# A fused attention and spatial-gating kernel: a new cost table and rank table for its list scheduler, some engines chosen by it, and weights converted in PSUM

## The chip, the cores and the metric

The kernel runs on one core of a Trainium2 chip. The core has TensorE (PE, matmuls into PSUM), VectorE (DVE), ScalarE (ACT), GpSimd (POOL) and SyncE (SP, which here issues every load and store). The metric is the time of one execution on the device in microseconds. Times before: 559.58 us as the median of three runs, from 556.43 to 561.42.

## The reference

Inputs are q, k and v of 4 batches x 8 heads x 768 tokens x 64, and the weights of an MLP with a spatial gate. Everything is float32 on the reference's side; some weights arrive as float64.

```python
def _attn_ref(q, k, v, n_global, n_local):          # 8 global keys, a window of 96
    scores = scale * np.matmul(q, k.transpose(0, 1, 3, 2))
    ...
    keep = is_global | is_local
    ...
    scores = np.where(keep, scores + bias, -1e9)     # bias = -slope[h] * distance
    a = np.exp(scores - np.max(scores, axis=-1, keepdims=True))
    return np.matmul(a / (np.sum(a, axis=-1, keepdims=True) + 1e-09), v)

def _moe_ref(x, w_in, w_spatial, b_spatial, w_out):  # x: 4 x 768 x 512
    h = np.maximum(x @ w_in, 0.0)                    # 512 -> 1024
    u, v = h[..., :512], h[..., 512:]
    v_n = (v - mu) / np.sqrt(var + 1e-06)            # over the last axis
    v_s = np.einsum('ts,bsd->btd', w_spatial, v_n) + b_spatial[None, :, None]
    return (u * v_s) @ w_out
```

## The kernel before

Work is cut into 24 blocks of 128 tokens, six to a batch. A block's attention (`scores` and `values`) needs only the block's own keys, those of the block before it, and up to 32 global keys which are copied over the first rows of a ring of keys (`kring`) and of values (`vring`). Per block and pair of heads: score matmuls into PSUM tile `s`; one DVE instruction adds the bias, evicts to `pr` and finds the extreme `mn`; ACT takes the exponential and its sum; DVE takes the reciprocal `rc`; POOL multiplies `pr` by it; PE transposes `pr` into `p`; ACT and DVE evict it as a high and a low part (`pth`); PE multiplies by the values into `ops`; ACT and DVE sum the parts into `c`, and ACT and POOL write the MLP's input as high part `xth` and low part `xtl`. Batch 0 does its attention matmuls in full float32 without such parts, each as two records in the profile.

The MLP works on chunks: `mlp_v` per 128 tokens (12 matmuls of 512 columns, ReLU, normalisation, parts `vnh` and `vnl`), `mlp_u` per 256 tokens (48 of 256 columns), `mlp_s` (72 of 256 columns, the spatial product; DVE adds `b_bc`, the gate product with `u` follows, then parts `gh` and `gl`) and `mlp_o` (24 of 512 columns, eviction, store). All its matmuls go to two PSUM banks, `m`. Each is a sum of three products of high and low parts.

The float64 weights are loaded raw and converted during batch 0 (`split_weights`, 12 tiles of 128x512): the bits of the upper word are rebuilt as a float by ACT and DVE, the lower word is added, ACT rounds the high part `hi`, and two more steps make `lo`. Before, this works in SBUF buffers (`raw`, `rawh`, `ev`) and the last two steps (`wsub`, `wadd`) run on POOL.

The program is not issued as it is written. A `Recorder` collects every call with its engine, what it reads and writes and a token (which step of which block or batch). `link` finds the dependences, `cost` gives each call a busy time and a time until its result counts, and `plan` is a list scheduler: at each step it takes the engine that is free first and gives it the ready call of the lowest rank. The rank is a due time from the token (`keys.get(token, default)`); before, `KEYS` is empty and the defaults hold. The engine of each kind of call stands in `CFG` ('a' ACT, 'v' DVE, 'p' POOL). The five queues that come out are then executed in order, each waiting for the others by semaphores. Every recorded call has line 35 in the profile (39 after the change), so one goes by tiles. Input loads and stores all pass through SP's one queue.

The program also holds a second, general path behind a branch that these inputs do not take.

Of the kernel before, what the change touches and what calls it, by code (L numbers as in the profile page):

```python
# [26 lines left out]
CFG = {'bias1': 'pppppppp', 'bias2': 'pppppppp', 'S': [['I01', 'A'], ['I00', 'T00', 'T01', 'A', 'V00', 'B00'], ['T02', 'T03', 'A', 'V01', 'U00'], ['T04', 'T05', 'A', 'V02'], ['Q00', 'Q01', 'A', 'V03', 'U01'], ['Q02', 'Q03', 'A', 'V04']], 'T': [['V15', 'U12', 'A'], ['G10', 'O10', 'A'], ['G11', 'O11', 'A'], ['G12', 'O12', 'V00', 'V01', 'U00', 'A'], ['V02', 'A'], ['V03', 'U01', 'A', 'V04']], 'END': ['V05', 'U02', 'G00', 'O00', 'G01', 'O01', 'G02', 'O02'], 'whi': 'a', 'wsub': 'p', 'wadd': 'p', 'wth': 'a', 'wtl': 'p', 'vhi': 'p', 'vlo': 'p', 'qhi': 'a', 'qlo': 'v', 'khi': 'a', 'klo': 'v', 'pth0': 'aaaa', 'x0h': 'aa', 'x0l': 'vv', 'pth': 'aaaa', 'xh': 'aa', 'c1': 'aa', 'xl': 'pppp', 'vnh': 'a', 'vnl': 'p', 'gm': 'pp', 'gh': 'aa', 'gl': 'pv', 'o': 'aa', 'norm0': 'pppppppp', 'norm': 'pppppppp', 'wp': 0, 'vrn': 'v', 'dup': 1, 'fold': '', 'xb': 1, 'div': 'a', 'rows': 'p', 'xf0h': 'a', 'xf0l': 'v', 'xdiv': 'v', 'xbh': 'a', 'xbl': 'p', 'b_rawqk': 1, 'b_ev': 3, 'b_raw': 1, 'b_pr': 10, 'b_pth': 2, 'b_c1': 3, 'b_ps_s': 2, 'b_ps_p': 2, 'b_ps_o': 2, 'b_ps_m': 2}  # L27
# [3 lines left out]
class Op:  # L31
    __slots__ = ("eng", "call", "args", "kw", "reads", "writes", "token", "num", "preds", "busy", "late", "port", "seq", "real")
# [21 lines left out]
class Recorder:  # L54
# [13 lines left out]

    def add(self, engine, call, args, kw):
        op = Op()  # L70
        op.eng, op.call, op.args, op.kw, op.token, op.real = engine.name, call, args, kw, self.now, engine.real
# [37 lines left out]
SIZE = {BF16: 1}  # L109
seen = {}  # L110
# [3 lines left out]
def extent(ap):  # L114

    t = ap.tensor
    key = t.name, ap.offset, tuple(tuple(x) for x in ap.ap), str(ap.dtype)
    if key not in seen:
        u = SIZE.get(ap.dtype, 2)
        row = 1  # L120
        for x in t.shape[1:]:
            row *= x
        row = row * SIZE.get(t.dtype, 2) // u
        p0, f0 = divmod(ap.offset, row)
        bits = 1
# [25 lines left out]

def cost(op):

    n = elements(op.writes[0])
    src = op.reads[0] if op.reads else op.writes[0]
    psum = any(in_psum(x) for x in op.reads + op.writes[:1])
    if op.eng == "tensor":
        if op.call == "transpose":
            return 109, 260, False
        n = elements(op.kw["rhs"])  # L160
        if op.kw["rhs"].dtype == F32:
            return 4 * max(n, 128) * .422, 4 * n * .422 + 170, False
        return {128: 111, 256: 120, 512: 228}[n], n * .417 + 175, False
    if op.eng == "sync":
        size = n * 4 * list(op.writes[0].ap)[0][1]
        return 560, 2200 + size * .0035, False
    if op.eng == "scalar":
        t = 60 + .82 * n if in_psum(src) else 110 + .83 * n
        if "accum_out" in op.kw:
            t = 80 + .83 * n + 280  # L170
        return t, t + 90, False
    if op.eng == "gpsimd":
        tt = op.call == "tensor_tensor"
        small = n <= 8
        if small:
            t = 540 if op.kw.get("op") == ALU.pow else 150
        elif tt:
            t = 142 + 2.17 * n
        elif isinstance(op.kw.get("scalar1"), bass.AP):
            t = 242 + .82 * n  # L180
        else:
            t = 155 + .84 * n
        return t, t + 90, True
    one = "accum_out" in op.kw or psum or op.call in ("bn_stats", "bn_aggr", "reciprocal", "tensor_reduce", "memset")
    if op.call == "reciprocal":
        t = 70 + 6.25 * n
    elif op.call in ("tensor_scalar", "tensor_copy") and not one:
        t = 68 + .53 * n
    elif op.call == "bn_stats":
        t = 70 + 1.04 * n  # L190
    elif op.call == "tensor_reduce":
        t = 70 + 1.04 * elements(src)
    else:
        t = 72 + 1.04 * n
    return t, t + 90, not one


def link(ops):

    wrote, used, bank = {}, {}, {}  # L200
    for op in ops:
        preds = set()
        for ap in op.reads:
            name, p0, p1, bits = extent(ap)
            for q0, q1, b, o in wrote.get(name, ()):
                if q0 < p1 and p0 < q1 and b & bits:
                    preds.add(o)
        for ap in op.writes:
# [22 lines left out]
        op.busy, op.late, op.port = cost(op)  # L231


def plan(ops, keys, trace=None):
# [4 lines left out]
    left = [len(op.preds) for op in ops]  # L239
    for op in ops:  # L240
# [3 lines left out]
    est = [0.0] * n  # L244
    free = {x: 0.0 for x in ("tensor", "vector", "scalar", "gpsimd", "sync")}
    port = 0.0
    wait = {x: [] for x in free}
    ready = {x: [] for x in free}
    for op in ops:
        if not left[op.num]:  # L250
            heapq.heappush(wait[op.eng], (0.0, op.num))
    start = [0.0] * n
    done = 0
    dma = 0.0
    while done < n:
        best = None
        for e in free:
            w, r = wait[e], ready[e]
            t = free[e]
            if not r and not w:  # L260
                continue
            if not r:
                t = max(t, w[0][0])
# [3 lines left out]
        while wait[e] and wait[e][0][0] <= t:  # L267
            x = heapq.heappop(wait[e])[1]
            heapq.heappush(ready[e], (rank[x], x))
        x = heapq.heappop(ready[e])[1]  # L270
        op = ops[x]
        if op.port:
            if port > t:
                others = []
                y = x
                while ops[y].port and ready[e]:
                    others.append(y)
                    y = heapq.heappop(ready[e])[1]
                if ops[y].port:
                    others.append(y)  # L280
                    y = others.pop(0)
                    t = max(t, port)
                for z in others:
                    if z != y:
                        heapq.heappush(ready[e], (rank[z], z))
                x, op = y, ops[y]
            if op.port:
                port = t + op.busy
        start[x] = t
        free[e] = t + op.busy  # L290
        end = t + op.late
        if e == "sync":
            dma = max(dma, t + 1200) + (op.late - 2200)
            end = dma + 1000
        done += 1
        for s in succs[x]:
            o = ops[s]
            at = t + op.busy if o.eng == e and e != "sync" else end + SLACK
            est[s] = max(est[s], at)
            left[s] -= 1  # L300
            if not left[s]:
                heapq.heappush(wait[o.eng], (est[s], s))
    if trace is not None:
        trace.extend(start)
    return sorted(ops, key=lambda op: (start[op.num], op.num))
# [4 lines left out]
SLACK = 200  # L310
KEYS = {}
# [3 lines left out]
def attn_then_spatial_gating_kernel(  # L315
# [90 lines left out]
    def hi_lo(src, hi, lo, e_hi, e_lo):  # L406
        split_hi(e_hi, hi, src)
        e_lo.tensor_tensor(out=lo, in0=src, in1=hi.bitcast(F32), op=ALU.subtract)

    def split_hi(e, hi, src):  # L410
        if e is nc.scalar:
            nc.scalar.activation(hi, src, AF.Copy)
        elif e is nc.gpsimd:
            nc.gpsimd.tensor_scalar(out=hi, in0=src, scalar1=1.0, scalar2=1.0, op0=ALU.mult, op1=ALU.mult)
        else:
            nc.vector.tensor_copy(out=hi, in_=src)
# [53 lines left out]
    def scaled(e, out, in_, by):  # L470
        if e is nc.scalar:
# [11 lines left out]
    def split_weights(src, hi, lo, tag, x):  # L483
# [40 lines left out]
        E("wsub").tensor_tensor(out=a, in0=a, in1=hi.bitcast(F32), op=ALU.subtract)  # L524
        E("wadd").tensor_tensor(out=lo, in0=a, in1=m, op=ALU.add)
# [36 lines left out]
    def copy(dst, src):  # L562
        nc.gpsimd.tensor_scalar(out=dst, in0=src, scalar1=1.0, scalar2=1.0, op0=ALU.mult, op1=ALU.mult)

    def prep(n):
# [75 lines left out]
    def scores(n, qq):  # L641
# [17 lines left out]
        for g in range(NP):  # L659
# [40 lines left out]
    def values(n):  # L700
# [19 lines left out]
        for g in range(NP):  # L720
# [39 lines left out]
            if CFG["xb"]:  # L760
                if g % 2:
# [7 lines left out]
                    if folded(n):  # L769
                        E("xdiv", g // 2).tensor_tensor(out=c1, in0=c1, in1=div[:, gs], op=ALU.mult)  # L770
# [11 lines left out]
            E("xl", g).tensor_tensor(out=xl[:, g, toks], in0=c1, in1=c2, op=ALU.add)  # L782
# [50 lines left out]
    def mlp_s(b, c):  # L833
# [3 lines left out]
        for fp in range(NF // 2):  # L837
# [9 lines left out]
            E("gm", fp).tensor_tensor(out=g, in0=g, in1=u[:, fs], op=ALU.mult)  # L847
# [191 lines left out]
```

## Time and profile before

| | before |
|---|---|
| median of three runs | 559.58 us (556.43 to 561.42) |
| the profiled execution | 561.15 us, its span 559.4 us |
| busy of the span | PE 88%, weight loads 77%, DVE 62%, ACT 55%, POOL 58% |
| granted TensorE clock, mean | 0.955 |
| moved by DMA | 65.48 MB, mean 117 GB/s |

The page's busy shares are means over a program that changes as it runs: batch 0 has the weight conversion beside attention, batches 1 to 3 have attention of one batch beside the MLP of the batch before, and the end is MLP alone. So the profile is read by windows, cut at the first score matmul of batch 1 (136 us) and the last attention matmul of batch 3 (497 us). Matmuls are pipelined, and their durations overlap; the start of one to the start of the next in a run without waits is the price of one.

### The profile page before, as it was taken

How to read it: one execution, taken by the hardware profiler on the slowest of the kernel's cores; microseconds unless marked ns; L12 is line 12 of the kernel's file. 1: busy time of each engine (PE TensorE's matmuls, PEld its weight loads, DVE VectorE, ACT ScalarE, POOL GpSimd, SP SyncE). 2: the span in 40 equal slices, each digit the busy share in tenths (PEclk: the TensorE clock that was granted, in tenths of full speed). 3: DMA queues.
4: the chain of work that ended last, by engine and by line, in shares of the span. 5: the costliest groups of instructions: out<-in, count | busy, mean ns of one | idle time of the engine just before them, and what ended most of it. 6: DMA issues, size and time to landing. Idle time of an engine off the chain costs nothing.

```text
span 559.4 us, 9755 instructions
## 1 busy us (share of the span) xinstructions
PE 493.3 (88%) x3116; PEld 432.1 (77%) x3116; DVE 349.6 (62%) x974; ACT 306.9 (55%) x800; POOL 322.1 (58%) x450
## 2 busy tenths in 40 slices
PE   4787879995987998998889999999889999899995
PEld 3465548875966896987878898897879889779884
DVE  5856989985575666477755655578776582751110
ACT  3737658544475566467746554677675654642111
POOL 4875889876634655266664655377756465253221
PEclk9858999997897998999998999999999999999998
DMA  7826620227545763456465375176456534000111
GB/s 203 239 59 155 193 78 23 72 66 178 150 104 142 182 176 95 125 124 154 111 170 134 94 194 159 44 178 162 115 128 193 134 90 127 11 1 1 39 38 44
DMA packets 68268, 65.48 MB, mean 117 GB/s; under 512 B 6672, under 2 KB 49936, under 8 KB 68208
## 3 DMA queue, kind: packets, MB, share of 16 engines
q1 hardware_dynamic: 68208, 64.78, 43.9%
q8 instruction: 26, 0.43, 0.3%
q14 instruction: 34, 0.28, 0.2%
HBM read 29.76 MB, written 6.68 MB: 65 GB/s over the span
## 4 chain that ended last, share of the span: by engine, by line
PE 52%; DVE 19%; POOL 8%; ACT 7%; DMA 5%; issue 5%; SPq 3%; POOLq 0%; ACTq 0%; DVEq 0%
PE m L35 34%; DVE c L35 8%; PE ops L35 7%; PE s L35 7%; PE p L35 4%; DVE pr L35 4%; SPq L35 3%; POOL pr L35 3%; DMA raw<-in_k_dram 2%; DVE ev L35 2%; ACT c L35 2%; DVE pth L35 1%; DVE raw L35 1%; ACT pr L35 1%; DMA u<-in_moe_w_in_dram 1%
## 5 line engine op out<-in xcount | busy, mean ns | idle before, releaser
L35 POOL TENSOR_SCALAR pr<-pr,rc 128x256 f32<-128x256 f32 (+1 forms) x192 | 96.6, 525 | 37.0 <-DVE rc L35 26.9
L35 ACT ACTIVATE pr<-pr,mn 128x256 f32<-128x256 f32 (+1 forms) x192 | 92.1, 481 | 35.1 <-DVE mn L35 34.6
L35 PE MATMUL s<-kring,q 128*128 128x256 f32 (+1 forms) x384 | 79.1, 336 | 27.1 <-DVE mn L35 12.5
L35 PEld LDWEIGHTS s<-kring,q 128*128 128x128 f32 x384 | 63.2, 211 | 38.9 <-DVE mn L35 19.1
L35 DVE CUSTOM_DVE_ANT_0 pr<-s,bias 128x256 f32<-128x256 f32 (+1 forms) x192 | 69.0, 397 | 30.5 <-PE s L35 27.1
L35 PE MATMUL ops<-pth,vring 128*128 128x256 f32 x352 | 75.5, 335 | 13.9 <-DVE c L35 4.6
L35 DVE TENSOR_TENSOR c<-ops,c 64x256 f32<-64x256 f32 x144 | 60.7, 422 | 29.7 <-ACT c L35 24.1
L35 PEld LDWEIGHTS ops<-pth,vring 128*128 128x128 f32 x352 | 55.2, 198 | 26.0 <-ACT pth L35 7.4
L35 ACT ACTIVATE pth<-p 128x512 fp32r<-128x512 f32 (+3 forms) x96 | 52.5, 561 | 37.9 <-PE p L35 37.2
L35 PE MATMUL p<-ident,pr 128*128 128x128 f32 x352 | 61.3, 283 | 4.2 <-POOL pr L35 4.0
L35 DVE TENSOR_TENSOR pth<-p,pth 128x512 fp32r<-128x512 f32 (+1 forms) x72 | 45.4, 643 | 30.9 <-ACT pth L35 29.7
L35 POOL TENSOR_TENSOR xtl<-c,xth 128x256 fp32r<-128x256 f32 x36 | 29.9, 832 | 49.9 <-ACT xth L35 46.0
L35 PEld LDWEIGHTS p<-ident,pr 128*128 128x128 f32 x352 | 43.3, 145 | 13.6 <-POOL pr L35 9.0
L35 POOL TENSOR_TENSOR ev<-ev,u 128x512 f32<-128x512 f32 x24 | 31.1, 1296 | 37.4 <-DVE ev L35 35.9
L35 PE MATMUL m<-w_t_h,vnh 128*128 128x256 f32 x288 | 47.3, 292 | 1.3 <-ACT u L35 1.3
L35 PE MATMUL m<-w_t_h,vnl 128*128 128x256 f32 x288 | 48.2, 289 | 0.0
L35 PE MATMUL m<-w_t_l,vnh 128*128 128x256 f32 x288 | 45.7, 288 | 0.0
L35 POOL TENSOR_TENSOR vnl<-ev,vnh 128x512 fp32r<-128x512 f32 x24 | 31.8, 1327 | 23.3 <-ACT vnh L35 21.9
L35 ACT ACTIVATE ev<-m 128x512 f32<-128x512 f32 (+1 forms) x49 | 28.6, 587 | 30.0 <-PE m L35 28.8
L35 ACT ACTIVATE c<-ops 64x256 f32<-64x256 f32 x72 | 27.3, 379 | 29.0 <-PE ops L35 27.9
L35 DVE TENSOR_TENSOR raw<-raw,rawh 128x512 fp32r<-128x512 f32 x36 | 33.3, 933 | 15.0 <-ACT rawh L35 14.4
L35 PEld LDWEIGHTS m<-w_t_h,vnh 128*128 128x128 f32 x288 | 40.0, 195 | 1.8 <-ACT u L35 1.7
(102 smaller groups left out, 1003.0 us busy)
## 6 DMA issues: line engine op xcount, KB each, us to landing
q<-rawh SPq DMA_DIRECT2D x72, 128.0 KB, 2.4
q<-raw SPq DMA_DIRECT2D x72, 128.0 KB, 2.4
out_dram<-ev SPq DMA_DIRECT2D x23, 256.0 KB, 2.7
raw<-in_v_dram SPq DMA_DIRECT2D x18, 256.0 KB, 2.6
raw<-in_q_dram SPq DMA_DIRECT2D x36, 128.0 KB, 2.9
raw<-in_k_dram SPq DMA_DIRECT2D x36, 128.0 KB, 3.0
kring<-rawh SPq DMA_DIRECT2D x36, 128.0 KB, 2.5
kring<-raw SPq DMA_DIRECT2D x36, 128.0 KB, 2.6
```

Source lines behind the costliest of these rows:

```text
L35: getattr(self.real, self.call)(*self.args, **self.kw)
```

## The change

Four things change, all in the scheduler's tables and in who does what.

1. `cost` has new constants for most kinds of calls, and a table `CROSS` gives the time from the end of a call on one engine to the start of its successor on another, per pair of engines, with a slack of 120 in place of a common 90 and 200.
2. `extent` widens each access to PSUM to whole banks (and all accesses to all partitions), so that two calls on one bank are ordered as the machine's semaphores will order them.
3. `Recorder.either` records a call with several ways of doing it (engine 'x' in `CFG`), and `plan` picks the engine that will end it first. With the indices that the code uses, four kinds of calls are so recorded: the gate product (`gm`), its low part (`gl`), the high part `vnh` and the high part of q (`qhi`). Other calls get another fixed engine: every second output copy (`o`) goes from ACT to DVE, eight bias tables (`bias2`) from POOL to ACT.
4. `wp` is 1: the weights are converted on a PSUM tile of the MLP's banks `m` in place of SBUF buffers; its last two steps are now on DVE, since POOL does not reach PSUM. `KEYS` has some 100 ranks in place of none.

The same calls are made with the same arithmetic, but for the order and the engine. The number of matmuls and of loads is the same.

```diff
-CFG = {'bias1': 'pppppppp', 'bias2': 'pppppppp', ..., 'whi': 'a', 'wsub': 'p', 'wadd': 'p', ..., 'qhi': 'a', ..., 'vnh': 'a', 'vnl': 'p', 'gm': 'pp', 'gh': 'aa', 'gl': 'pv', 'o': 'aa', ..., 'wp': 0, ...}
+CFG = {'kept': 'p', 'bias1': 'pppppppp', 'bias2': 'a', ..., 'whi': 'aaax', 'wsub': 'xx', 'wadd': 'v', ..., 'qhi': 'xv', ..., 'vnh': 'xvpa', 'vnl': 'p', 'gm': 'x', 'gh': 'aa', 'gl': 'x', 'o': 'vava', ..., 'wp': 1, ...}
...
+        if name.split("_")[0] in PSUM_NAMES:
+
+            bits = sum(BANK << x for x in range(0, bits.bit_length(), 1024) if bits >> x & BANK)
+        seen[key] = name, 0, P, bits
...
+CROSS = {
+    "tensor": {"vector": 205, "scalar": 225, "gpsimd": 255, "sync": 220},
+    "scalar": {"vector": 140, "gpsimd": 172, "tensor": 160, "sync": 125},
+    "vector": {"scalar": 125, "gpsimd": 168, "tensor": 142, "sync": 125},
+    "gpsimd": {"scalar": 72, "vector": 50, "tensor": 88, "sync": 70},
+}
...
+def reach(op, o, eng, end, stand):
+
+    if op.eng == "sync":
+        return end if eng == "sync" and op.num not in o.after else stand + 50 + SLACK
+    if op.eng == eng:
+        return stand + 95 if op.num in o.after and eng != "tensor" else end
+    return stand + CROSS[op.eng][eng] + SLACK
...
+            way, busy, late, shared = ways[y][e]
+            at = max(t, port) if shared else t
+            sooner = None
+            for f in ways[y]:
+                if f != e:
+                    b = ways[y][f]
+                    start = max(free[f], est[y][f], port if b[3] else 0.0)
...
+                    if start + b[1] < at + busy and (sooner is None or start < sooner):
+                        sooner = start
...
-SLACK = 200
-KEYS = {}
+SLACK = 120
+KEYS = {('P', 0): 0.8, ('S', 0): -0.6, ('P', 1): 1.0, ('A', 0): -0.2, ('S', 1): 0.4, (0, 'T', 0): 3.0, ...}
...
-        E("wsub").tensor_tensor(out=a, in0=a, in1=hi.bitcast(F32), op=ALU.subtract)
-        E("wadd").tensor_tensor(out=lo, in0=a, in1=m, op=ALU.add)
+        two(E("wsub"), a, a, hi.bitcast(F32), ALU.subtract)
+        two(E("wadd"), lo, a, m, ALU.add)
...
-            E("gm", fp).tensor_tensor(out=g, in0=g, in1=u[:, fs], op=ALU.mult)
+            two(E("gm", fp), g, g, u[:, fs], ALU.mult)
```

With `wp` at 1, the conversion takes the branch of `split_weights` that stood there unused (its lines 494 to 511).

More of the change, by code (lines that the diff above doesn't have):

```diff
@@ L28, with take @@
 NLMAX = 97
 class Op:
-    __slots__ = ("eng", "call", "args", "kw", "reads", "writes", "token", "num", "preds", "busy", "late", "port", "seq", "real")
+    __slots__ = ("ways", "eng", "call", "args", "kw", "reads", "writes", "token", "num", "preds", "after", "busy", "late", "port", "seq", "real")
+    def take(self, way):
+        engine, self.call, self.args, self.kw = self.ways[way]
+        self.eng, self.real = engine.name, engine.real
     def issue(self):
@@ L67, in token, with either @@
         self.now = now
+    def either(self, *ways):
+        if not self.open:
+            engine, call, args, kw = ways[0]
+            return getattr(engine, call)(*args, **kw)
+        self.add(*ways[0])
+        self.ops[-1].ways = ways
     def add(self, engine, call, args, kw):
         op = Op()
-        op.eng, op.call, op.args, op.kw, op.token, op.real = engine.name, call, args, kw, self.now, engine.real
+        op.ways = ((engine, call, args, kw),)
+        op.token = self.now
+        op.take(0)
         outs = [kw[x] for x in ("out", "accum_out") if x in kw]
@@ L109 @@
 SIZE = {BF16: 1}
+BANK = (1 << 1024) - 1
 seen = {}
@@ L149 @@
 ON_DRAM = ("in", "out", "vg")
+CROSS = {
[4 more added lines that the diff above has]
+}
 def cost(op):
-    n = elements(op.writes[0])
-    src = op.reads[0] if op.reads else op.writes[0]
+    out = op.writes[0]
+    n = elements(out)
+    src = op.reads[0] if op.reads else out
@@ L181, in cost @@
         else:
             t = 155 + .84 * n
-        return t, t + 90, True
+        return t, 0, True
     one = "accum_out" in op.kw or psum or op.call in ("bn_stats", "bn_aggr", "reciprocal", "tensor_reduce", "memset")
     if op.call == "reciprocal":
[L186 to L194, printed above, removed]
@@ L195, in cost @@
-    return t, t + 90, not one
+        return 70 + 6.25 * n, 85, False
+    if op.call in ("tensor_scalar", "tensor_copy") and not one:
+        return (75 + 1.04 * n if out.dtype == I32 else 70 + .53 * n), 0, True
+    if op.call in ("tensor_reduce", "bn_stats"):
+        return 70 + 1.04 * elements(src), 0, False
+    if op.call == "bn_aggr":
+        return 99, 0, False
+    return (190 if parts < P else 74) + 1.04 * n, 0, not one
 def link(ops):
@@ L207, in link @@
                     preds.add(o)
+        op.after = set(preds)
         for ap in op.writes:
@@ L242, in plan @@
             succs[x].append(op.num)
-    rank = [(keys.get(op.token[0], op.token[1]), op.num) for op in ops]
[L244 to L252, printed above, removed]
+        mine = {}
+        for w in range(len(op.ways)):
+            op.take(w)
+            mine[op.eng] = (w,) + cost(op)
+        ways.append(mine)
+    rank = [(keys.get(op.token[0], op.token[1]), op.num) for op in ops]
+    est = [dict.fromkeys(x, 0.0) for x in ways]
+    names = ("tensor", "vector", "scalar", "gpsimd", "sync")
+    free = dict.fromkeys(names, 0.0)
+    port = dma = 0.0
+    wait = {x: [] for x in names}
+    ready = {x: [] for x in names}
+    begun = [None] * n
+    for x in range(n):
+        if not left[x]:
+            for e in ways[x]:
+                heapq.heappush(wait[e], (0.0, x))
     done = 0
-    dma = 0.0
     while done < n:
         best = None
-        for e in free:
+        for e in names:
             w, r = wait[e], ready[e]
-            t = free[e]
+            while r and begun[r[0][1]] is not None:
+                heapq.heappop(r)
+            while w and begun[w[0][1]] is not None:
+                heapq.heappop(w)
             if not r and not w:
                 continue
-            if not r:
-                t = max(t, w[0][0])
+            t = free[e] if r else max(free[e], w[0][0])
             if best is None or t < best[0]:
@@ L266, in plan @@
         t, e = best
[L267 to L270, printed above, removed]
+        w, r = wait[e], ready[e]
+        while w and w[0][0] <= t:
+            x = heapq.heappop(w)[1]
+            if begun[x] is None:
+                heapq.heappush(r, (rank[x], x))
+        passed, x = [], None
+        while r:
+            y = heapq.heappop(r)[1]
+            if begun[y] is not None:
+                continue
+            way, busy, late, shared = ways[y][e]
[5 more added lines that the diff above has]
+                    start = max(free[f], est[y][f], port if b[3] else 0.0)
+                    start += sum(ways[z][f][1] for k, z in ready[f] if z != y and k < rank[y] and begun[z] is None and len(ways[z]) == 1)
+                    if start + b[1] < at + busy and (sooner is None or start < sooner):
+                        sooner = start
+            if sooner is not None:
+                heapq.heappush(w, (max(sooner, t) + 1.0, y))
+                continue
+            if at > t and x is None and not passed:
+                passed.append(y)
+                continue
+            if at > t:
+                passed.append(y)
+                continue
+            x = y
+            break
@@ L271, in plan @@
+        if x is None:
+            if not passed:
+                continue
+            x = passed.pop(0)
+        for y in passed:
+            heapq.heappush(r, (rank[y], y))
         op = ops[x]
+        way, op.busy, op.late, op.port = ways[x][e]
+        op.take(way)
         if op.port:
[L273 to L291, printed above, removed]
+            t = max(t, port)
+            port = t + op.busy
+        begun[x] = t
+        free[e] = end = t + op.busy
+        stand = end + op.late
         if e == "sync":
-            dma = max(dma, t + 1200) + (op.late - 2200)
-            end = dma + 1000
+            dma = max(dma, t + 1200) + (op.late - 2050)
+            stand = dma + 1400
         done += 1
@@ L296, in plan @@
         for s in succs[x]:
-            o = ops[s]
-            at = t + op.busy if o.eng == e and e != "sync" else end + SLACK
-            est[s] = max(est[s], at)
+            for f in est[s]:
+                est[s][f] = max(est[s][f], reach(op, ops[s], f, end, stand))
             left[s] -= 1
             if not left[s]:
-                heapq.heappush(wait[o.eng], (est[s], s))
+                for f in est[s]:
+                    heapq.heappush(wait[f], (est[s][f], s))
     if trace is not None:
-        trace.extend(start)
@@ L330, in attn_then_spatial_gating_kernel, with on_psum, any_of @@
     nc = Recorder(bare)
-    EN = {"a": nc.scalar, "v": nc.vector, "p": nc.gpsimd}
-    def cp(e, out, in_):
-        if e is nc.scalar:
+    EN = {"a": nc.scalar, "v": nc.vector, "p": nc.gpsimd, "x": None}
+    def on_psum(ap):
+        return nc.open and in_psum(ap)
+    def any_of(way, *others):
+        nc.either(way, *[x for x in others if x])
+    def cp(e, out, in_):
+        if e is None:
+            any_of(
+                (nc.scalar, "activation", (out, in_, AF.Copy), {}),
+                (nc.vector, "tensor_copy", (), dict(out=out, in_=in_)),
+                None if on_psum(in_) else
+                (nc.gpsimd, "tensor_scalar", (), dict(out=out, in0=in_, scalar1=1.0, scalar2=1.0, op0=ALU.mult, op1=ALU.mult)),
+            )
+        elif e is nc.scalar:
             nc.scalar.activation(out, in_, AF.Copy)
@@ L406, in hi_lo, with two @@
     def hi_lo(src, hi, lo, e_hi, e_lo):
[L407 to L414, printed above, removed]
+        cp(e_hi, hi, src)
+        two(e_lo, lo, src, hi.bitcast(F32), ALU.subtract)
+    def two(e, out, in0, in1, op):
+        kw = dict(out=out, in0=in0, in1=in1, op=op)
+        if e is None:
+            any_of((nc.vector, "tensor_tensor", (), kw), None if on_psum(in0) else (nc.gpsimd, "tensor_tensor", (), kw))
         else:
-            nc.vector.tensor_copy(out=hi, in_=src)
+            e.tensor_tensor(**kw)
     def even(t):
```

67 lines of the change are left out of this document (40 added, 27 removed).

## The prediction

> **What bounds the kernel now.** I read the page's busy shares first, then the same shares in three stages cut where the program changes character: up to the first score matmul of batch 1, from there to the last attention matmul of batch 3, and the rest. The stages' rows give the stretch and its length, the busy time (and instructions) of PE, weight loads, DVE, ACT and POOL, the granted clock, the DMA share and GB/s.
>
> ```profile
> PE 493.3 (88%) x3116; PEld 432.1 (77%) x3116; DVE 349.6 (62%) x974; ACT 306.9 (55%) x800; POOL 322.1 (58%) x450
> ...
> 0.00:136.00 136.00, 104.83 (x498) 82.01 (x498) 105.19 (x274) 76.89 (x195) 104.43 (x133) 0.90 0.45 124
> 136.00:497.00 361.00, 333.29 (x2244) 300.32 (x2245) 233.30 (x681) 217.79 (x583) 200.31 (x300) 0.97 0.51 130
> 497.00:559.40 62.40, 55.20 (x376) 49.76 (x375) 11.09 (x20) 12.27 (x23) 17.39 (x18) 0.98 0.08 28
> ```
>
> A busy PE is not a PE at its rate, so I price its work by rows where matmuls follow each other without a wait, of the timeline (a row's start to the next row's) and of the chain of waits (start, duration, pieces):
>
> ```profile
> 502.16 1.09 PE L35 MATMUL m<-w_in_l,xth 128*128 128x512 f32 x4
> 503.10 1.09 PE L35 MATMUL m<-w_in_h,xtl 128*128 128x512 f32 x4
> ...
> 504.26 0.64 PE L35 MATMUL m<-xtl,w_in_h 128*128 128x256 f32 x4
> 504.74 0.52 PE L35 MATMUL m<-xth,w_in_l 128*128 128x256 f32 x3
> ```
> ```profile
> 57.12 1.74 PE ops L35 x8
> ...
> 94.00 0.66 PE p L35 x6
> 94.65 5.91 PE m L35 x38
> ...
> 120.70 1.48 POOL raw L35
> 122.25 1.62 POOL w_out_l L35
> ...
> 126.32 1.31 POOL rawh L35
> 127.69 1.35 POOL w_out_l L35
> ...
> 133.50 2.47 DMA kring<-raw
> 136.01 1.12 PE s L35 x4
> ```
>
> So 512 columns cost 0.235 us (0.94/4), 256 cost 0.119 (0.48/4), 128 cost 0.11 (0.66/6), and a record of a full-precision 256-column matmul of batch 0 costs 0.2175. Counted by the program's order, stage 1 holds 16 records of 128 and 168 of 256 columns in full precision, 88 transposes, 72 of 512 and 154 of 256: 83.1 us of work in 136. Stage 2 holds 312 of 128, 1526 of 256 and 414 of 512: 312.4 in 361, or 86.5%. The tail holds 78 of 512 and 288 of 256: 52.5 in 62.4. In all 448 us of work in 559.4. PE sets the floor; the 111 us above it are what an order can win: 53, 49 and 10.
>
> Stage 1 is not PE's. DVE and POOL are both busy 105 us of 136, and the chain near its end runs through POOL's weight splits up to the load that starts batch 1. Stage 2 is near PE's rate in its best windows and far from it in others:
>
> ```profile
> 240.00:280.00 40.00, 35.90 (x258) 32.34 (x257) 30.34 (x103) 29.47 (x86) 26.88 (x43) 1.00 0.56 137
> 320.00:360.00 40.00, 39.26 (x263) 35.59 (x263) 21.49 (x60) 22.16 (x54) 19.80 (x31) 1.00 0.54 142
> 440.00:480.00 40.00, 38.75 (x263) 35.00 (x261) 21.25 (x54) 20.82 (x51) 19.76 (x31) 1.00 0.45 119
> ```
>
> The first of these is full of attention (DVE 30.3, ACT 29.5), the others of MLP.
>
> **What moves between engines.** Groups by shape: count, busy us, mean ns, idle before.
>
> ```profile
> L35 POOL TENSOR_TENSOR ev<-ev,u 128x512 f32<-128x512 f32 x24 | 31.1, 1296 | 37.4 <-DVE ev L35 35.9 <-DVE rc L35 0.8 <-DMA raw<-in_q_dram 0.7
> L35 POOL TENSOR_TENSOR gl<-ev,gh 128x512 fp32r<-128x512 f32 x12 | 16.4, 1365 | 12.1 <-ACT gh L35 12.1
> L35 DVE TENSOR_TENSOR gl<-ev,gh 128x512 fp32r<-128x512 f32 x12 | 8.8, 730 | 6.2 <-ACT gh L35 6.2
> L35 DVE TENSOR_TENSOR ev<-m,b_bc 128x512 f32<-128x512 f32 x24 | 16.5, 689 | 38.8 <-PE m L35 38.6
> L35 DVE TENSOR_SCALAR ev<-ev,mv,rs 128x512 f32<-128x512 f32 x24 | 15.2, 635 | 11.2 <-POOL rs L35 10.9
> L35 ACT ACTIVATE vnh<-ev 128x512 fp32r<-128x512 f32 x24 | 15.1, 628 | 9.9 <-DVE ev L35 9.9
> L35 POOL TENSOR_TENSOR rawh<-rawh,w_in_h 128x512 f32<-128x512 f32 x4 | 5.8, 1452 | 2.6 <-ACT w_in_h L35 2.6
> ...
> L35 POOL TENSOR_TENSOR w_out_l<-rawh,ev 128x512 fp32r<-128x512 f32 x2 | 2.7, 1351 | 0.2
> L35 DVE TENSOR_SCALAR raw<-raw 128x512 int32<-128x512 int32 x12 | 9.6, 802 | 0.4
> ...
> L35 DVE SCALAR_TENSOR_TENSOR ev<-gh,raw 128x512 f32<-128x512 uint32 x2 | 1.5, 729 | 0.1
> L35 DVE TENSOR_TENSOR raw<-raw,rawh 128x512 fp32r<-128x512 f32 x36 | 33.3, 933 | 15.0 <-ACT rawh L35 14.4
> ```
>
> POOL loses 23 gate products (23 x 1.296 = 29.8 us), 12 low parts (16.4) and the 24 subtracts and adds of the weights (eight groups of which the first and last are shown, 33.5); it gains 9 copies of 512 (nearest: its 128x512 tensor-scalar groups, about 0.7 each, 6). It ends near 249 from 322. DVE gains the 23 products (0.73 each, as its low part: 16.8), the 12 low parts (8.8), the 24 weight steps (0.689, as the two-input step that reads PSUM: 16.5), 12 copies of output tiles from PSUM (0.689: 8.3) and 12 high-part copies (0.635: 7.6), 58 in all. Its six other weight steps sum to 59.1 us over 14 groups (first and last shown), 4.9 a tile; on PSUM operands at 0.689 they would be 4.1, so between nothing and 9.5 us goes: I take 5. DVE ends near 403. ACT loses 12 output copies, 12 high parts and 9 more (33 x 0.6 = 20) and gains 8 small ones.
>
> In the pair 933 against 689 ns, the slower subtract has both inputs in SBUF and the faster has one in PSUM. The Trainium skill, "GPSIMD Engine Reference", § 1 Specifications, says that GpSimd shares its SBUF interface with VectorE and contends with DVE instructions that have two SBUF inputs; the trace's pair agrees. By that rule the 35 products and low parts, both inputs in SBUF, would cost 0.933 and not 0.73, 7 us more on DVE; put wholly on the path they make the forecast 540.
>
> **What moves in the order.** SP's queue at the start, before and then after (q and kring are the first block's scores, u the raw w_in):
>
> ```order
> L35 DMA nraw<-in_n_local_dram 128x2
> L35 DMA q_0_94<-in_q_dram 64x4x128
> L35 DMA kring_96<-in_k_dram 64x4x128
> L35 DMA q_0_94<-in_q_dram 64x4x128
> L35 DMA kring_96<-in_k_dram 64x4x128
> L35 DMA vring_112<-in_v_dram 128x512
> ```
> ```order
> L39 DMA nraw<-in_n_local_dram 128x2
> L39 DMA vring_112<-in_v_dram 128x512 x2
> L39 DMA u_113<-in_moe_w_in_dram 128x1024
> L39 DMA u_116<-in_moe_w_in_dram 128x1024
> L39 DMA u_119<-in_moe_w_in_dram 128x1024
> L39 DMA q_0_94<-in_q_dram 64x4x128
> L39 DMA kring_96<-in_k_dram 64x4x128
> ```
>
> Five loads now stand before the first q, two of 256 KB and three of 512 KB (tile, count, KB each, us to landing):
>
> ```profile
> u<-in_moe_w_in_dram SPq DMA_DIRECT2D x8, 512.0 KB, 5.5
> ...
> vring<-in_v_dram SPq DMA_DIRECT2D x6, 256.0 KB, 3.5
> ```
>
> That is 2.1 MB, or 9 us at the 225 GB/s of the first 20 us (row below). DVE at the start, after (before, the scores' evictions to pr follow the bias row at once):
>
> ```order
> L39 TENSOR_SCALAR bias_85<-ev_99 128x128 x8
> ...
> L39 SCALAR_TENSOR_TENSOR m_114<-m_114,raw_0_115 128x512
> L39 TENSOR_SCALAR m_117<-u_116 128x512
> L39 SCALAR_TENSOR_TENSOR m_114<-ev_97,m_114 128x512
> L39 TENSOR_SCALAR rawh_0_118<-m_117 128x512
> L39 TENSOR_SCALAR raw_0_115<-m_114 128x512
> L39 TENSOR_TENSOR m_114<-m_114,w_in_h 128x512
> L39 SCALAR_TENSOR_TENSOR ev_97<-u_113,raw_0_115 128x512
> L39 SCALAR_TENSOR_TENSOR m_117<-m_117,rawh_0_118 128x512
> L39 ISA pr_103,mn_100<-s_102,bias_85 128x128
> ```
>
> Ten weight steps (of tiles u_113 and u_116, on PSUM tiles m_114 and m_117; eight are shown) now precede the first eviction. The first gate product of batch 0's MLP, in the middle of batch 1's attention, on POOL before and then on DVE after (ev is the gate, u the ReLU half, c and xtl belong to attention):
>
> ```order
> L35 TENSOR_TENSOR ev_97<-ev_97,u_119 128x512
> L35 TENSOR_TENSOR gl_167<-ev_97,gh_166 128x512
> L35 TENSOR_TENSOR xtl_139<-c_0_164,xth_138 128x2x128
> L35 TENSOR_TENSOR ev_98<-ev_98,u_119 128x512
> L35 TENSOR_TENSOR xtl_139<-c_1_165,xth_138 128x2x128
> ```
> ```order
> L39 TENSOR_TENSOR ev_97<-m_114,b_bc 128x512
> L39 TENSOR_TENSOR c_0_163<-ops_93,c_0_163 64x256
> L39 TENSOR_TENSOR ev_97<-ev_97,u_119 128x512
> L39 ISA pr_110,mn_126<-s_102,bias 128x256
> L39 ISA mn_126 128x1
> L39 ISA pr_111,mn_126<-s_102,bias 128x256
> ```
>
> The product leaves POOL, where attention's xtl stood behind it, and stands on DVE, where the eviction of attention's scores (pr) stands behind it: 0.73 us that PE's next scores can wait for, in place of 1.3 us that the next block's xtl could.
>
> **The sum, stage by stage.** The start, by its windows and by the chain:
>
> ```profile
> 0.00:20.00 20.00, 11.17 (x41) 8.24 (x41) 12.20 (x67) 8.95 (x28) 11.91 (x35) 1.00 0.89 225
> 20.00:40.00 20.00, 15.36 (x41) 10.30 (x42) 15.20 (x36) 11.88 (x29) 14.81 (x19) 0.60 0.40 124
> ```
> ```profile
> 4.89 0.18 DVE nf L35
> ...
> 9.55 0.20 DVE pr L35
> ```
>
> Stage 1. The order after holds 71 matmuls of 512 and 110 of 256 here: PE's work falls to 77.7, and PE does not set it. DVE does: 105.2 + 16.5 (weight steps) + 1.3 (two copies) - 5 = 118 busy. Before, DVE idled 31 us of the stage, 12.6 of it by 40 us. After, the first eviction comes at about 17 (9.55 plus ten steps of about 0.7; the loads' 9 us run beside them), but DVE works on weights while it waits; the first 5 us wait for the sizes whatever the order. POOL's 33.5 us of weights, the end of the old chain, are gone from it. I take 10 us of DVE idle: 128. The ends are 123 (the first 5 alone) and 149 (all 31 stay).
>
> Stage 2. The order holds 312 of 128, 1508 of 256 and 391 of 512, 304.9 us of PE work. At the old 86.5% that is 352; at the 97% of the two best windows (39.0 of 40) 314. What can raise it: 73 us less on POOL, half of it here, a product of 0.73 where 1.296 stood, MLP work held back for attention's holes. Against it: DVE carries 233 plus about 35. That is 81% of 331, and in its densest shown window DVE had 76%, so it is loaded but not full. I take 331, near the middle.
>
> Tail. 102 of 512 and 350 of 256, 65.4 us of work; the 9.9 us over it were mostly the last chain, in which only the product shortens, by 0.6:
>
> ```profile
> 547.16 0.69 DVE L35 TENSOR_TENSOR ev<-m,b_bc 128x512 f32<-128x512 f32 x1 [3.56 <-PE m L35]
> ...
> 547.93 1.29 POOL L35 TENSOR_TENSOR ev<-ev,u 128x512 f32<-128x512 f32 x1 [0.92 <-DVE ev L35]
> ...
> 549.25 0.63 ACT L35 ACTIVATE gh<-ev 128x512 fp32r<-128x512 f32 x1 [3.61 <-POOL ev L35]
> ```
>
> I take 74 (65.4 + 8.6), from 72 to 76. The 12.9 us of PE work that stages 1 and 2 hand to the tail cost there what they cost anywhere.
>
> 128 + 331 + 74 = 533, against the profiled span of 559.4. That execution took 561.15 in all, 1.8 outside the span and 1.6 above the median of 559.58; so the span's number stands for the median's too: 533.
>
> **Rivals.** First: the holes only move. Stage 2 keeps 86.5% since its waits are of the attention chain (score, exponential, reciprocal, normalise), whose steps keep their engines. Then 128 + 352 + 74 = 554; with stage 1 at 130, 556: within 1%. For it: attention's window 240 to 280 is the worst shown, and the change barely shortens that chain. Against: POOL, which normalises, is freed.
>
> Second, on the other side: the late start. If the first block starts at 17 and its blocks then run one behind another while DVE weaves in weight steps, PE stays sparse and at a lower clock, as between 20 and 40 (0.60 granted), and DVE's old idle time stays: stage 1 takes 149. With stage 2 at its old rate, 149 + 352 + 74 = 575. It decides from a stage 1 over about 140, if stage 2 gains little. The Trainium skill, "TensorE: Matmul & The Clock Gate", Part 1, says that an idle window of about 3.4 us halves the PE clock; the 0.60 agrees. For it: the five loads. Against: PE has 58 us to spare in stage 1.
>
> Third: DVE becomes the bound of stage 2. It would need no idle to speak of at 268 us; 268/0.76 is 353, so this ends as the first rival does. That engines are not chosen anew is ruled out by the order, where 23 of 24 products stand on DVE.
>
> **Chances.** Forecast, stages 1 and 2 both gaining: 0.72. First and third rival: 0.16. Second: 0.12. The range reaches from 123 + 314 + 72 = 509 to 558, which takes in the first rival and leaves out the late start and little else. A measurement of this kernel tells about 1% from no change: faster by more, 0.73; within, 0.15; slower, 0.12.
>
> **What would show it.** Right: the first batch-1 score at 123 to 135 us; POOL's busy time near 250 and DVE's near 400; stage 2 (from that score to the last ops matmul) at 320 to 340; PE's matmul time in all unchanged in count and work. Wrong: the first score eviction after 20 us with PE's clock under 0.8 up to 60; waits of PE for DVE's evictions of s growing; products on DVE at 0.93. A faster stage 1 alone would leave the time near 550.

## The result, and the profile after

The changed kernel takes 518.55 us (median of four runs, 517.67 to 519.95), against 560.5 us for the kernel before on the same chip (556.43 to 562.84). The ratio is 0.926, with a 95% interval from 0.920 to 0.932. The profiled execution took 517.67 us, its span 515.9. Of the four runs of one kernel below, the one with engines and PSUM alone, one was in a slower state and is left out of its median.

First the page's busy shares and the granted clock in 40 slices, then the windows at the same three cuts (first score matmul of batch 1, last attention matmul, end), with the columns of the prediction's table:

```profile
PE 467.0 (91%) x3116; PEld 422.2 (82%) x3116; DVE 377.8 (73%) x1057; ACT 283.5 (55%) x775; POOL 236.0 (46%) x392
...
PEclk9998889979999999999999999999999999999999
```
```profile
0.00:133.20 133.20, 93.68 (x453) 75.33 (x454) 104.54 (x299) 73.65 (x196) 53.10 (x98) 0.94 0.46 129
133.20:445.00 311.80, 307.75 (x2214) 286.48 (x2213) 250.10 (x718) 196.06 (x553) 172.02 (x279) 1.00 0.58 149
445.00:515.90 70.90, 65.52 (x452) 60.40 (x450) 23.20 (x40) 13.74 (x26) 10.88 (x16) 0.99 0.07 25
```

Call the length of a stage less its PE work (counts of matmuls by the prediction's rates) its **holes**. Before, the three stages had 52.9, 48.6 and 9.9 us of holes; after, 55.5 (133.2 - 77.7), 6.9 (311.8 - 304.9) and 5.5 (70.9 - 65.4). All PE work together is 448 us in both. So of the 43.5 us that left the span, 41.7 left the holes of stage 2, and stage 1 has 2.6 more than before. Its own length fell by 2.8 us, and it holds 5.4 us less PE work.

What the holes of stage 2 were, the waits say. What PE waited for, before (us in total, times, longest), in stage 2:

```profile
PE s L35 <- DVE mn L35: 8.1, 13, 1.3
PE m L35 <- DVE ev L35: 5.8, 3, 2.4
PE s L35 <- DMA kring<-raw: 5.6, 1, 5.6
PE ops L35 <- DVE c L35: 4.6, 10, 0.9
PE ops L35 <- DVE pth L35: 3.3, 7, 0.7
PE m L35 <- ACT xth L35: 2.8, 2, 1.5
PE m L35 <- DVE gl L35: 1.2, 4, 0.4
PE ops L35 <- ACT u L35: 1.0, 2, 0.5
PE p L35 <- POOL pr L35: 0.6, 1, 0.6
```

And after, in stage 2:

```profile
PE m L39 <- DVE ev L39: 1.1, 2, 0.8
PE s L39 <- DVE mn L39: 1.0, 2, 0.8
PE m L39 <- ACT ev L39: 0.9, 1, 0.9
PE s L39 <- DMA kring<-raw: 0.6, 2, 0.4
PE p L39 <- POOL pr L39: 0.3, 1, 0.3
PE ops L39 <- DVE pth L39: 0.2, 1, 0.2
```

The first list sums to 33.0 us, the second to 4.1. But the 5.6 us for a load in the first list lie just before the cut, from 130.4 to 136.0 us, and are a hole of stage 1; so the waits within stage 2 went from 27.4 to 4.1. Another part of the old holes is the clock. Two windows of before, the first right behind the 5.6 us wait for a load that ends stage 1:

```profile
136.00:143.20 7.20, 7.19 (x33) 7.19 (x34) 3.69 (x21) 4.64 (x18) 4.00 (x7) 0.50 0.48 137
143.20:150.40 7.20, 7.20 (x60) 7.05 (x59) 3.79 (x8) 2.71 (x7) 3.13 (x7) 0.98 0.79 197
```

PE looks busy in all of both, but at a granted clock of 0.50 the first holds 33 matmuls, the second 60. Over the 361 us of that stage the mean clock was 0.97, so about 10.8 us of full clock were lost; after, the mean is 1.00. Waits (27.4 to 4.1) and clock (10.8 to nothing) account for up to 34.1 of the 41.7 us; up to, since a wait that fell into a stretch of low clock is in both. What made the rest is not shown by these two views. The wait of 5.6 us thus cost twice: once itself, in stage 1, and once in the clock behind it, in stage 2.

### The profile page after: what moved, and what is told of

It is laid out like the page before. It is cut to its first block, busy times and chain, and to the rows that moved or that the text cites. A ratio compares the mean times of both kernels' runs of the same rounds, so it can differ in the third digit from the quotient of the medians.

```text
span 515.9 us, 9756 instructions
## 1 busy us (share of the span) xinstructions
PE 467.0 (91%) x3116; PEld 422.2 (82%) x3116; DVE 377.8 (73%) x1057; ACT 283.5 (55%) x775; POOL 236.0 (46%) x392
## 4 chain that ended last, share of the span: by engine, by line
PE 62%; DVE 16%; ACT 7%; DMA 6%; issue 4%; POOL 2%; SPq 1%; ACTq 0%; DVEq 0%; POOLq 0%
PE m L39 45%; PE s L39 7%; PE ops L39 7%; PE p L39 4%; DVE ev L39 4%; DVE m L39 3%; ACT pr L39 3%; DVE pr L39 2%; DMA raw<-in_q_dram 2%; DVE raw L39 2%; SPq L39 1%; DVE c L39 1%; DVE pth L39 1%; DMA gl<-in_moe_w_spatial_dram 1%; DMA gh<-in_moe_w_out_dram 1%
## 5 line engine op out<-in xcount | busy, mean ns | idle before, releaser
L39 POOL TENSOR_SCALAR pr<-pr,rc 128x256 f32<-128x256 f32 (+1 forms) x192 | 91.9, 498 | 55.1 <-DVE rc L39 46.8
L39 PE MATMUL s<-kring,q 128*128 128x256 f32 (+1 forms) x384 | 72.0, 323 | 22.1 <-DMA kring<-in_k_dram 14.4
L39 PEld LDWEIGHTS s<-kring,q 128*128 128x128 f32 x384 | 59.8, 202 | 29.6 <-issue 15.9
L39 PE MATMUL ops<-pth,vring 128*128 128x256 f32 x352 | 65.3, 316 | 10.5 <-ACT xth L39 5.5
L39 PE MATMUL p<-ident,pr 128*128 128x128 f32 x352 | 52.6, 274 | 0.9 <-POOL pr L39 0.8
L39 ACT ACTIVATE ev<-m 128x512 f32<-128x512 f32 (+1 forms) x37 | 21.6, 584 | 44.6 <-PE m L39 42.2
L39 PE MATMUL m<-w_t_h,vnl 128*128 128x256 f32 x288 | 43.1, 282 | 0.0
L39 PE MATMUL m<-w_t_l,vnh 128*128 128x256 f32 x288 | 42.6, 281 | 0.0
L39 PEld LDWEIGHTS m<-w_t_h,vnl 128*128 128x128 f32 x288 | 37.9, 189 | 0.0
L39 PEld LDWEIGHTS m<-w_t_l,vnh 128*128 128x128 f32 x288 | 37.7, 188 | 0.0
```

Source lines behind the costliest of these rows:

```text
L39: getattr(self.real, self.call)(*self.args, **self.kw)
```

## The experiments

Two accounts were to be told apart. The prediction's: engines are relieved (POOL first), so that PE's partners answer sooner, and ranks help. Its rival: the order alone does it, because ranks bring MLP work, which PE can always do, to where attention leaves holes. A third, which came up with the first results: neither does anything without the other.

Here the combinations of the parts in one table. "Holes" are those of stage 1, stage 2 and tail in the profiled execution, with PE work counted from that kernel's own order; medians can lie some 4 to 5 us from the profiled execution, so a difference of a few us in holes between two kernels is within that. "Planner" stands for costs, crossing times, whole banks and the new loop of `plan` that uses them.

| what is in the kernel | median us | ratio to before (95%) | holes us |
|---|---|---|---|
| before | 558 to 560 | 1 | 52.9, 48.6, 9.9 |
| planner alone | 554.74 | 0.993 (0.990 to 0.997) | 55.6, 35.2, 10.0 |
| ranks alone | 557.67 | 1.001 (0.997 to 1.004) | 47.9, 48.7, 9.5 |
| engines and PSUM alone | 577.15 | 1.030 (1.024 to 1.037) | 69.0, 51.7, 12.1 |
| planner, engines, PSUM; no ranks | 559.45 | 1.001 (0.998 to 1.004) | 65.7, 33.7, 11.5 |
| planner, ranks | 543.07 | 0.975 (0.970 to 0.980) | 56.3, 27.8, 9.1 |
| planner, ranks, PSUM; old engines | 538.13 | 0.962 (0.958 to 0.967) | 61.6, 18.5, 8.6 |
| planner, ranks, engines; no PSUM | 530.14 | 0.949 (0.945 to 0.953) | 48.7, 26.4, 5.3 |
| all four | 518.55 | 0.926 (0.920 to 0.932) | 55.5, 6.9, 5.5 |

Every kernel of it is planned anew by its own scheduler, so an undo changes the order as well as what it names.

**All but the ranks.**

```diff
-KEYS = {('P', 0): 0.8, ('S', 0): -0.6, ...}
+KEYS = {}
```

> The changed kernel with an empty rank table; new costs, crossing times, whole banks, engine choices and the conversion in PSUM stay. If the ranks make the order that keeps PE fed, most of the gain goes: 545 to 556 us, stage 2 back over 330. If the crossing times and the relief of POOL make it, it stays at 520 to 530.

It takes 559.45 us: without ranks the other three parts gain nothing. Stage 2 of this kernel, by windows:

```profile
144.70:496.40 351.70, 330.21 (x2295) 303.85 (x2295) 264.45 (x731) 205.69 (x560) 185.38 (x288) 0.98 0.52 133
```

POOL is relieved here much as in the full change (243 us busy in the whole program, 236 in the full change, 322 before), and the holes of stage 2 are still 33.7 us, nearly the 35.2 of the planner alone. So relief of POOL is not the cause by itself.

**The old engines back.**

```diff
-'bias2': 'a', 'qhi': 'xv', 'vnh': 'xvpa', 'gm': 'x', 'gl': 'x', 'o': 'vava'
+'bias2': 'pppppppp', 'qhi': 'a', 'vnh': 'a', 'gm': 'pp', 'gl': 'pv', 'o': 'aa'
```

> The changed kernel with the engines of before for the gate product, its low part, the high parts of v and q, the output copies and the second bias tables; ranks, costs and the conversion in PSUM stay. If the order makes the gain: 518 to 526. If it is POOL's relief: 540 or more, with waits behind the gate product on POOL.

538.13 us, next to the second branch: the engines are worth 19.6 us within the full change. Without them stage 2 has 11.6 us more of holes, stage 1 has 6.1 and the tail 3.1. The waits behind the product on POOL are ACT's: its `gh` waits 18.6 us for it in stage 2. PE's own waits there sum to 9.9 us, against 4.1 in the full change. Six kinds of calls went back at once; which of them counts was not tried.

**The weights not in PSUM.**

```diff
-'whi': 'aaax', 'wsub': 'xx', 'wadd': 'v', 'wp': 1
+'whi': 'a', 'wsub': 'p', 'wadd': 'p', 'wp': 0
```

> The changed kernel with the weights converted in SBUF and their last two steps on POOL, as before. If the conversion in PSUM matters only to stage 1: stage 1 grows from 133 to about 140, time 522 to 528, stage 2 stays near 312. If DVE's two extra steps per tile cost more than POOL's relief gives: no change or a gain of a few us.

530.14 us, 11.6 more than the full change. Its windows, stages 1 and 2:

```profile
0.00:143.00 143.00, 108.49 (x576) 88.98 (x577) 108.73 (x284) 76.61 (x202) 105.10 (x128) 0.96 0.44 124
143.00:457.30 314.30, 296.56 (x2088) 271.56 (x2088) 244.11 (x714) 193.61 (x547) 163.08 (x268) 0.99 0.57 147
```

POOL is back at 105 us in stage 1. By length it is this stage that grew, by 9.8 us, near the 140 of the first branch, and stage 2 by 2.5. Yet the holes aren't there: this stage 1 does 94.3 us of PE work in its 143, with fewer holes than the full change (48.7 against 55.5). They are in stage 2, 26.4 us of holes against 6.9, although POOL has less to do there (163.1 us against 172.0). What differs is the order: 16.6 us of PE work that the full change still has for stage 2 are done in stage 1 (the tail's work is the same within 0.5 us). That fits filler used too early; it is not shown by itself.

**Engines and PSUM in the kernel before**, with its planner and no ranks:

```diff
-'bias2': 'pppppppp', 'gm': 'pp', 'gl': 'pv', 'o': 'aa', 'wp': 0
+'bias2': 'a', 'gm': 'vv', 'gl': 'vv', 'o': 'va', 'wp': 1
```

> The kernel of before, its planner and empty ranks, with the gate product and its low part on DVE, every second output copy on DVE, the second bias tables on ACT, and the conversion in PSUM. If POOL's relief is the main cause: 525 to 540. If the order is: 550 to 562, with stage 2 still near 86% of PE's rate.

577.15 us, 3% slower. Nearly the same moves (`qhi` and `vnh` stay on ACT here) are worth 24.5 us with the new planner and the ranks (543.07 to 518.55). Of the 21.4 us that they add to the span of the profiled execution here, 16.1 are holes in stage 1. The timelines of PE and of DVE (start, duration, instruction, idle before) show one of them:

```profile
40.47 2.07 PE L35 MATMUL s<-kring,q 128*128 128x256 f32 x4 [19.40 <-DVE mn L35]
```
```profile
38.31 0.70 DVE L35 SCALAR_TENSOR_TENSOR m<-ev,m 128x512 f32<-128x512 f32 x1
39.04 0.69 DVE L35 TENSOR_SCALAR rawh<-m 128x512 int32<-128x512 int32 x1
39.65 0.41 DVE L35 CUSTOM_DVE_ANT_0 pr<-s,bias 128x256 f32<-128x256 f32 x1
39.98 0.08 DVE L35 DVE_READ_ACCUMULATOR2_ANT mn<- 128x1 f32 x1
```

PE's next scores need the `s` tile that DVE evicts to `pr`, and DVE has a row of weight steps queued ahead of it, 0.69 us each: PE stands for 19.4 us. In this order, the weight chain, with its last steps moved from POOL to DVE, stands in front of attention. The kernel that has all but the ranks has the same wait, 15.2 us at its longest; the full change, with ranks, has 4.0.

**The ranks in the kernel before.**

```diff
-KEYS = {}
+KEYS = {('P', 0): 0.8, ('S', 0): -0.6, ...}
```

> The kernel of before, its planner, costs, engines and conversion, with the new rank table alone. If the ranks by themselves make the order that keeps PE fed: 525 to 540. If they work only with the crossing times and costs they stand beside: 550 or more.

557.67 us, no change: 48.7 us of holes in stage 2, as before. The rival account, order by ranks alone, falls as the first did.

**Planner and ranks; planner alone.** The first undoes both edits of `CFG` above, the second the ranks as well.

> The changed kernel's planner and ranks, with the engines and the conversion of before: the order alone. The two undone apart cost 20 and 12 us; if they add up: about 550. If the order is the main cause and either of them is enough to free POOL: 538 to 545.

> The changed kernel's costs, crossing times and whole banks, with no rank table and the engines and conversion of before. The ranks alone gave nothing (e5), ranks and planner together 14 us (e6). If the two need each other: 553 to 562. If the planner alone carries those 14 us and the ranks only the rest: 540 to 548.

543.07 and 554.74 us. The two parts undone together cost 24.5 us, less than the 31.2 of the two undone apart. The profile of the planner alone has 13.4 us less of holes in stage 2 (48.6 to 35.2), but its median gains only 0.7%: the profile is of its fastest run (550.55 us), that of before of one of its longer runs (561.15), so some 6 us of this are the choice of execution. With it, the ranks gain 2.1% (554.74 to 543.07), where with the old costs they gained nothing. In stage 2 the holes then go from 27.8 to 26.4 by the engines alone, to 18.5 by PSUM alone, and to 6.9 by both: what each is worth depends on the other.

**Which ranks.** Of the 111 entries of `KEYS`, 77 are for attention and 34 for single steps of the MLP and of its weights. The first of these two kernels has the 77 alone; the second has them and a plain rule for the MLP, each step due one block later:

```diff
-        nc.token((b, tok[0], j), n + .5)
+        nc.token((b, tok[0], j), n + (1.5 if tok[0] in 'VUGO' else .5))
```

> The changed kernel with the 77 ranks of attention's steps alone; the 34 ranks of MLP and weight steps are left out. If what counts is that scores and the loads of q and k stand some 0.7 block earlier: 518 to 530. If it is the MLP held back in reserve: 540 or more, with a tail near 63 us as without ranks.

> As e7 (attention's 77 ranks alone), but every MLP step due one block later, by one rule in place of 34 ranks. If a reserve of MLP work for PE is what the 34 ranks give: 518 to 532, with a tail over 70 us and stage 2 under 315. If it takes the single ranks: 545 as e7.

548.06 us (0.982, from 0.978 to 0.987) and 538.31 us (0.965, from 0.958 to 0.973); the second lies between its two branches. Without the 34 MLP ranks the change is 29.5 us slower; the plain rule wins back 9.8 of them. Stage 2 of the first kernel, then stage 2 and tail of the second:

```profile
138.50:488.30 349.80, 331.15 (x2300) 303.91 (x2299) 257.68 (x733) 201.30 (x561) 180.16 (x285) 0.98 0.52 133
```
```profile
142.80:454.00 311.20, 302.67 (x2153) 278.91 (x2153) 246.62 (x713) 194.06 (x545) 171.60 (x272) 0.99 0.57 148
454.00:533.70 79.70, 74.36 (x507) 68.39 (x505) 27.92 (x49) 15.04 (x28) 15.05 (x22) 0.99 0.06 22
```

The rule halves the holes of stage 2 (31.4 to 16.2 us). The work it pushes into the tail (74.4 us there, against 51.0) costs nothing extra, since the tail runs at 93%. The rest of stage 2's holes, and about 9 us of holes in stage 1, go only with the single ranks; how these do it is open.

**The rule without ranks**, the same line with `KEYS` empty:

> As e1 (no rank table), but every MLP step due one block later. If the reserve alone feeds PE: 530 to 545. If scores must also come earlier than the values' half: 550 to 560, as e1.

548.52 us (0.981, from 0.973 to 0.989), between the two branches and 10.9 better than without it: the rule is worth about the same with and without the attention ranks. Holding MLP work back is a cause by itself beside the new planner, engines and PSUM, and a part of the whole; without those it was not tried.

**Another slack** on every crossing:

```diff
-SLACK = 120
+SLACK = 140
```

> The changed kernel with the slack per crossing at 140 in place of 120, which plans the whole order anew and means little in itself. If the ranks carry the gain in a way that survives another order: 516 to 524. If they fit one order by chance: 530 or more.

522.09 us (0.937, from 0.933 to 0.941). The gain survives this one other plan, less 3.5 us.

**The first scores first.** The full change, but the first block's q and k are loaded ahead of the values and raw weights, as before:

```diff
-KEYS = {('P', 0): 0.8, ...
+KEYS = {('P', 0): 0.0, ...
```

> The changed kernel with one rank changed, so that the first block's q and k are loaded before the two loads of v and the three of the weights, as before. If the late start (first matmul at 14.4 in place of 7.7 us) is on the path of stage 1: stage 1 at 125 to 130, time 511 to 516. If the weights' conversion on DVE is: 518 to 526.

517.94 us (0.926, from 0.919 to 0.934): the same as the full change. Its stage 1 by windows, PE's two longest waits in it, and the same two waits in the full change:

```profile
0.00:132.50 132.50, 96.96 (x453) 76.60 (x454) 102.71 (x298) 74.84 (x197) 53.40 (x98) 0.90 0.47 129
```
```profile
PE m L39 <- DVE w_in_l L39: 10.7, 1, 10.7
PE s L39 <- DMA kring<-in_k_dram: 7.8, 1, 7.8
```
```profile
PE s L39 <- DMA kring<-in_k_dram: 14.4, 1, 14.4
PE m L39 <- DVE w_in_l L39: 5.9, 1, 5.9
```

PE starts 6.6 us sooner, and then waits 4.8 us longer for the first weights that DVE has converted. So the late start costs nothing here: it was off the path.

## Why the prediction was right, and where not

**Sign and place were right, the size too small.** 533 us was forecast, 518.55 came. By its own terms, 128 + 331 + 74 became 133.2 + 311.8 + 70.9: stage 1 missed by +5.2, stage 2 by -19.2, the tail by -3.1, so the first miss hid a part of the second. Of the prediction's own signs, stage 2 at 320 to 340 us did not come.

**The step that was mis-sized is stage 2's rate.** The prediction put 304.9 us of PE work between 86.5% and the 97% of the two best windows, and took 331, near the middle, "81% of 331" being DVE's load. Measured: 311.8 us, 97.8%, better than the end called best. The best windows of before held MLP; here attention's windows are as dense. The prediction gave reasons for a rise and none for the middle. It left out that a filled hole also keeps the clock up (up to 10.8 of the 41.7 us).

**Which part raises it was only half right.** Of the three reasons that the prediction gave, the relief of POOL and the shorter product stood first. The runs with engines and PSUM alone (+3%) and with all but the ranks (no change) show that these gain nothing without the order; ranks alone gain nothing either. Only the third, work held back for attention's holes, has a price of its own, about 10 us by the plain rule, and that beside the new planner, engines and PSUM.

**Stage 1, 128, was 133.2.** PE's work there was read rightly (77.7), DVE's load too high (118 for 104.5) and its idle time too low (10 for 28.7, which is nearly the 31 of before). That the idle time would go since DVE "works on weights while it waits" is the part that failed: DVE is busy where it was to be, and idle later. A part of the load's miss is in the adding: the stage's DVE instructions last 125.2 us if summed one by one, 118.1 before, but DVE is busy 104.5, since an instruction that follows at once begins before the one ahead ends. In the timeline (start, duration) two weight steps stand 0.60 us apart and last 0.68 and 0.69:

```profile
16.22 0.68 DVE L39 SCALAR_TENSOR_TENSOR ev<-u,raw 128x512 f32<-128x512 uint32 x1
16.82 0.69 DVE L39 SCALAR_TENSOR_TENSOR m<-m,rawh 128x512 int32<-128x512 int32 x1
```

The prediction added such durations to a busy time. Four windows of the full change:

```profile
0.00:20.00 20.00, 4.08 (x17) 3.75 (x18) 13.63 (x62) 7.32 (x24) 6.53 (x21) 1.00 0.83 225
20.00:40.00 20.00, 16.79 (x73) 12.03 (x72) 18.07 (x53) 15.08 (x44) 13.38 (x21) 1.00 0.71 183
40.00:60.00 20.00, 12.05 (x48) 8.53 (x48) 19.36 (x50) 14.39 (x36) 9.41 (x12) 0.91 0.65 212
60.00:80.00 20.00, 15.11 (x82) 13.14 (x83) 15.21 (x42) 8.20 (x22) 6.65 (x14) 0.83 0.13 39
```

DVE has 37.4 of the 40 us from 20 to 60, and 15.2 of 20 after. What bounds the stage now was not tried: the chain goes through DVE's weight steps and two loads of other weights, which is an argument and no experiment.

**Tail, 74, was 70.9**: the work was right, 65.4; the 9.9 us over it fell to 5.5, where 8.6 was taken.

**The rivals.** *The holes only move*: refuted by stage 2. *The late start*: its first half came true, the first score eviction stands at 17.4 us as forecast (9.55 before). But the clock of the first 60 us is 1.00, 1.00 and 0.91, not 0.60, and the start moved back gains nothing, which fits PE's spare time in stage 1, named there against it. *DVE as the bound of stage 2*: DVE is at 80% there, and PE is not held by it even where DVE is full:

```profile
260.00:300.00 40.00, 39.78 (x296) 37.53 (x296) 37.79 (x102) 27.35 (x77) 21.70 (x35) 1.00 0.66 166
```

37.8 of 40 on DVE, beside 39.8 on PE. The 76% that the prediction divided by was the densest window it showed, not a limit.

**Busy times**: POOL 236.0 for 249, DVE 377.8 for 403. The prices, by groups of the full change (count, busy us, mean ns, idle before):

```profile
L39 DVE TENSOR_TENSOR ev<-ev,u 128x512 f32<-128x512 f32 x23 | 18.3, 797 | 0.5
...
L39 DVE TENSOR_SCALAR raw<-m 128x512 int32<-128x512 int32 x12 | 8.3, 688 | 0.2
L39 DVE SCALAR_TENSOR_TENSOR m<-ev,m 128x512 f32<-128x512 f32 x12 | 8.2, 687 | 0.1
L39 DVE COPY ev<-m 128x512 f32<-128x512 f32 x12 | 8.2, 682 | 4.9 <-PE m L39 4.9
...
L39 DVE CAST vnh<-ev 128x512 fp32r<-128x512 f32 x11 | 4.7, 428 | 0.2
```

The steps on PSUM cost what was taken, 0.68 to 0.69. The copies of high parts from SBUF cost 0.43, not 0.635. The product came out at 0.797, between the 0.73 of the row and the 0.933 of the pair (see the last section).

## What to carry to other kernels

Subtract PE's work at its measured rate from each stage: the holes say where an order can win, and a hole that a wait leaves may be paid again in the clock behind it. Moving a call to a less busy engine is worth nothing, or less, until the order says what stands behind it in that queue; so try engines, costs and ranks together, and don't judge one of them alone (here 1.03, 0.993 and 1.001, and 0.926 together). Work that no one waits for yet did best here when kept for the stretch that has holes, although the end then grew.

## What the hardware showed that was not expected

**A DVE instruction with two SBUF inputs costs by what POOL does.** The groups of the full change on DVE, first in stage 2, then in the tail:

```profile
L39 DVE TENSOR_TENSOR ev<-ev,u 128x512 f32<-128x512 f32 x17 | 14.2, 834 | 0.3
L39 DVE TENSOR_TENSOR ev<-m,b_bc 128x512 f32<-128x512 f32 x18 | 12.4, 687 | 6.7 <-PE m L39 6.6
```
```profile
L39 DVE TENSOR_TENSOR ev<-ev,u 128x512 f32<-128x512 f32 x6 | 4.2, 692 | 0.2
L39 DVE TENSOR_TENSOR ev<-m,b_bc 128x512 f32<-128x512 f32 x6 | 4.1, 691 | 19.4 <-PE m L39 19.4
```

The product reads two SBUF tiles: 834 ns in stage 2, where POOL is busy 172 us of 312, and 692 in the tail, where it is busy 11 of 71. The step before it reads one tile in PSUM and one in SBUF, and costs 687 and 691: the same. The Trainium skill, "GPSIMD Engine Reference", § 1 Specifications, says that GpSimd contends with DVE instructions of two SBUF inputs; this trace agrees, with 142 ns on 692.

The stages differ in their loads too, so the trace was read instruction by instruction. The full change has 83 DVE instructions of this size with two SBUF inputs (product, its low part, attention's subtract). The 36 with no POOL instruction beside them took 670 to 694 ns, and 15 of these, which ran while the DMA engines were over half busy, 685 in the mean: so it is not the loads. The 47 with POOL beside them took 659 to 1759 ns, 872 in the mean; 24 of them are over 720. The longest product, and the POOL instruction that began 0.07 us ahead of it:

```profile
378.40 1.76 DVE L39 TENSOR_TENSOR ev<-ev,u 128x512 f32<-128x512 f32 x1
```
```profile
378.33 1.28 POOL L39 TENSOR_TENSOR vring<-raw,vring 128x512 fp32r<-128x512 f32 x1
```

So the mean price of such a step fell with POOL's work: attention's subtract on DVE went from 933 to 813 ns, with no change of its own.

**PE is at a half clock for a while after its work is back.** The 7.2 us behind the wait of 5.6 us, shown above, ran at 0.50 with PE busy throughout. In windows of 1 us, the stretches at 0.50 that touch stage 2 of before last about 10.2 us (from 133.2, in that wait), 6.8 (from 174.2), 3.4 (from 215.2) and 3.4 (from 293.7); the last two begin behind or in a wait of 2.4 us for DVE. Stage 2 after has none.
